# Gated mix of an S5 scan and an H3 convolution on one core: half-width trigonometric tables, another order of the first chunk, and the last rows by column halves

## The chip, the cores and the metric

The kernel runs on one core of a Trainium2 chip. The metric is the device time of one execution in microseconds. A run lists one time per execution; the time of a kernel is the median of its runs. Beside the timed runs there is one profiled execution, with the start, the duration and the waits of every instruction.

The core has five engines that run side by side and meet through semaphores: PE (matrix products, with PEld for its weight loads), DVE (elementwise), ACT (activation functions and scaled copies), POOL (small setup, and the issue of accumulating DMAs) and SP (issue of the other DMAs). Each engine takes its instructions in the order in which they were written down for it.

## What is computed

Inputs have 2048 rows (time) and 1024 columns (features), in bf16. Two branches are computed from the same `x` and mixed by a gate per row:

```python
g = sigmoid((x * gate_w).sum(-1, keepdims=True))

# branch A: a diagonal complex state space, P = 1024 states
Lam = Lambda_re + 1j * Lambda_im
Lam_bar = exp(exp(log_dt) * Lam)
B_bar = ((Lam_bar - 1) / Lam)[:, None] * (B_re + 1j * B_im)
Bu = einsum("bld,pd->blp", x, B_bar)
h[t] = Lam_bar * h[t - 1] + Bu[t]
a = 2 * einsum("blp,dp->bld", h, C_re + 1j * C_im).real + x * Dskip

# branch B: four taps on k, times v, a long convolution with ssm_k, a skip, times x
kv = (sum over t of shifted k * shift_k) * v
y = irfft(rfft(kv, 2L) * rfft(ssm_k, 2L))[:L] + kv * ssm_D
b = x * y

out = g * a + (1 - g) * b
```

## The kernel before, in words

All five engines' orders are written out by hand. Every operation goes through `put` (line 98) and so has line 100 in the profile; groups are told apart by the names of their tiles.

**Branch B** goes through 8 chunks `c` of 128 features. For a chunk, `load("kT", c)`, `load("v", c)` and `load("kn", c)` fetch `k` transposed, `v`, and the filter `ssm_k` transposed. `dgs` builds four diagonal matrices from the tap weights (tile `dg`, one buffer); for chunk 0 they are `dg0`, on DVE. `taps` (or `first_times_v` for chunk 0) makes 64 small matmuls against them in two PSUM halves, `times_v` multiplies by `v` into `ks`. `mirror` reverses `ks` in time on PE, from which DVE makes an even part `ev` and an odd part left in `ks`. Then `fwd_K` and `fwd_V` transform the filter and `ks` by matmuls against tables of cosines and sines: `KC` and `KS_` (four 128-row tiles by 512 columns) for the filter, `CF` and `SF` (two by 512) for `ks`. The 512 columns are frequencies and are taken as four blocks `fi` of 128. `overlap` and `products` (or `mid_products`) form the spectrum `G` on DVE, with some sums done by accumulating DMAs (`gather`). `inverse` turns `G` back (PSUM tiles `psz` and `low`) and stores the chunk in DRAM (`cv_scr`). A chunk's inverse is done in the next chunk's turn. `add_skip` adds `ssm_D` to the first row of the filter tile `kn`.

**Branch A**: `state_params` computes the small columns from `log_dt` and `Lambda`; its four steps are put between other work by `step(sp)`. `Bu` steps (PSUM `bu`) are spread over the chunks to fill PE. After the chunks come 16 scan steps (`scan`), with `Cy_g` (PSUM `psy`) for the output products.

**Tables.** A table's value is the cosine or sine of 2 pi times a product of a row number and a column number. `kernel_table(h)` makes the product `a` for 256 columns of all four tiles, removes whole turns by adding and subtracting `MAGIC` (`r`), and ACT takes sine, absolute value and cosine. `kA = kernel_table(0)` comes first of all, `kB = kernel_table(1)` later, in steps between the work of chunk 0. `CF` and `SF` come from `hf` and `rqf` at full width.

**Start.** ACT issues the six small row DMAs (tap weights `skr`, three A parameters `prow`, `gwr`, `sD`). PE turns these rows to columns by small matmuls into the PSUM tile `p`, with idle products (`raise_clock`, tile `raised`) around them. SP issues, in this order: `kT` of chunk 0 first half, `v` first half, `kT` second half, `v` second half, `kn` of chunk 0. PSUM holds four tiles of this size in all, given out in turn, so a matmul may have to wait until ACT or DVE has read an older tile.

**Buffers of loads.** `kT`, `v` and `kn` of all chunks share four buffers, so a load waits until an older chunk's tile has been used. SP issues in order, so a load that waits holds those behind it. `load_BT(0, ...)`, the first B matrices of branch A, stand behind `kT` of chunk 2.

**End.** The last four row tiles share one loop (lines 1235 to 1247). Each has a PSUM tile of two halves of 512 columns; for each tile PE makes the last eight matmuls, and then DVE adds the gate's part and SP stores 1024 columns. For one of them ACT scales and DVE adds; the last tile's matmuls go by halves and it is stored in two halves.

Of the kernel before, what the change touches and what calls it, by code (L numbers as in the profile page):

```python
# [9 lines left out]
ALU = mybir.AluOpType  # L10
# [10 lines left out]
def kernel(  # L21
# [26 lines left out]
    nc = tc.nc  # L48
# [126 lines left out]

    nc.scalar.dma_start(out=skr, in_=B_shift_k.rearrange("(j p) k -> j p k", p=128))
    for i, ap in enumerate((A_log_dt, A_Lambda_re, A_Lambda_im)):
        nc.scalar.dma_start(out=prow[i * ND:(i + 1) * ND, :], in_=ap.rearrange("(j p) -> j p", p=128))
    nc.scalar.dma_start(out=gwr, in_=gate_w.rearrange("(j p) -> j p", p=128))
    pih = consts.tile([128, 1], F32, name="pih")  # L180
# [5 lines left out]
    put("act", nc.scalar.activation, out=one, in_=magic, func=ACT.Sin, scale=0.0)  # L186
    nc.scalar.dma_start(out=sD, in_=B_ssm_D.rearrange("(o d) -> o d", o=1))

# [30 lines left out]
    put("pool", nc.gpsimd.memset, kT0[:, 0:PAD], 0.0)  # L219
    for h in range(2):  # L220
        hs, ns = slice(h * S // 2, (h + 1) * S // 2), slice(h * NT // 2, (h + 1) * NT // 2)
        load_t(kT0[:, PAD + hs.start:PAD + hs.stop], kf[hs, 0:128])
        move(v0[:, ns, 0], vf.rearrange("(n p) d -> p n d", p=128)[:, ns, 0:128])
    lds["kT", 0], lds["v", 0] = kT0, v0[:, :, 0]
    load("kn", 0)

# [39 lines left out]
    colk_i = iota_i32([128, 4], [[128, 4]], 0, 1, "colk")  # L266
    fr_i = iota_i32([128, 512], [[4, 512]], 1, 0, "fr_")
    ident = consts.tile([128, 128], BF16, name="ident")
# [27 lines left out]
    ts(colk, colk_i, 1.0 / 2048.0, None, ALU.mult)  # L296
    fr_ = room[:, 0:512]
    copy(fr_, fr_i)

    def kernel_table(h):  # L300

        hs = slice(h * 256, (h + 1) * 256)
        a, r = early([128, 4, 256], F32, "ka"), early([128, 4, 256], F32, "kr")
        for q in range(4):
            ts(a[:, q], fr_[:, hs], colk[:, q:q + 1], None, ALU.mult)
            ts(r[:, q], fr_[:, hs], colk[:, q:q + 1], MAGIC, ALU.mult, ALU.add)
            if q == 1:
                yield
        put("dve", V.scalar_tensor_tensor, out=flat(r), in0=flat(r), scalar=-MAGIC, in1=flat(a), op0=ALU.add,
            op1=ALU.subtract)  # L310
        yield
        act(KS_[:, :, hs], r, func=ACT.Sin, scale=-TWO_PI)
        act(a, r, func=ACT.Abs)
        yield
        act(KC[:, :, hs], a, func=ACT.Sin, bias=pih, scale=-TWO_PI)

    pcol = consts.tile([128, 3 + KS, ND], F32, name="pcol")
    gwb = consts.tile([128, ND], BF16, name="gwb")
    psp = ps2([128, 2, 512], "p")
    raise_clock(3)  # L320
    for k in range(KS):
        mm(psp[:, 1, k * ND:(k + 1) * ND], skr[:, :, k], ident[32:32 + ND, 32:32 + ND], True, True)
    raise_clock(5)
    mm(psp[:, 0, 0:3 * ND], prow, ident[64:64 + 3 * ND, 64:64 + 3 * ND], True, True)
    mm(psp[:, 1, KS * ND:(KS + 1) * ND], gwr, ident[32:32 + ND, 32:32 + ND], True, True)
    raise_clock(2)
    kA = kernel_table(0)
    steps(kA, 2)
    hf, rqf = early([128, 1024], F32, "h"), early([128, 1024], F32, "rq")
    for mt in range(2):  # L330
        ts(hf[:, mt * 512:mt * 512 + 512], fr_, colm[:, mt:mt + 1], None, ALU.mult)
    copy(pcol[:, 3:], psp[:, 1, 0:KS * ND].rearrange("p (i j) -> p i j", j=ND))
    dg0 = ks_pool.tile([128, KS, 128], BF16, name="dg", bufs=1)
    for k in range(KS):
        ts(dg0[:, k], ident, pcol[:, 3 + k, 0:1], None, ALU.mult)

    def dgs(c, on_dve=False):
# [179 lines left out]
    def first_times_v(c, dg):  # L517

        kT, v = lds.pop(("kT", c)), lds.pop(("v", c))
        ks = kss[c] = ks_pool.tile([128, 4, 4, 128], BF16, name="ks")  # L520
        for h in range(2):
            tt(of_blocks(ks, h), by_block(tap_sums(kT, dg, h)), by_block(v[:, 8 * h:8 * h + 8]), ALU.mult)
            yield
        lo = mirror(c)
        yield
        e = eo_pool.tile([128, 2, 4, 128], BF16, name="ev")
        tt(e, ks[:, 2:4], lo, ALU.subtract)
        tt(ks[:, 2:4], ks[:, 2:4], lo, ALU.add)
        eos["v", c] = e, ks[:, 2:4]

    def times_v(c):

        ks, v = kss[c], lds.pop(("v", c))
        tt(ks, ks, v.rearrange("p (b q) d -> p q b d", q=4), ALU.mult)
        yield
        lo = eo_pool.tile([128, 2, 4, 128], BF16, name="lo", tag="lo", bufs=2)
        act(lo, mirror(c), func=ACT.Copy)
        yield
        e = eo_pool.tile([128, 2, 4, 128], BF16, name="ev")
        tt(e, ks[:, 2:4], lo, ALU.subtract)  # L540
        if c == 1:
            tt(ks[:, 2:4], ks[:, 2:4], lo, ALU.add)
        else:
            gather(ks[:, 2:4], lo)
        eos["v", c] = e, ks[:, 2:4]
# [352 lines left out]

    def Cy_g(tb, tl, ps, g, last, by_half=False):
        t0 = HP + tl * 128  # L900
        tsl = slice(t0, t0 + 128)
        order = [(j, c, dh) for j in range(2) for c in range(2) for dh in range(2)]
        for j, c, dh in sorted(order, key=lambda o: o[2]) if by_half else order:
            mm(ps[dh], hbs[tb, g][:, c, j, tsl], CT[2 * g + j][:, c, dh * 512:(dh + 1) * 512],
               g == 0 and j == 0 and c == 0, last and j == 1 and c == 1)
# [26 lines left out]
    def finish(t_, ps=None):  # L932
# [4 lines left out]
        if t_ < NT - 4:  # L937
            ga = gas.pop(t_)
            gather(ga, xr)
            yield  # L940
        elif ps is None:
            yield
            ga = gas.pop(t_)
            tt(ga, ga, xr, ALU.add)
        else:
            yield
            ga = a_room(t_)
            for o, i in ps:
                put("dve", V.scalar_tensor_tensor, out=ga[:, o], in0=i, scalar=gcols[:, t_:t_ + 1], in1=xr[:, o],
                    op0=ALU.mult, op1=ALU.add)  # L950
                if len(ps) > 1:
                    move(of[rows, o], ga[:, o])
            if len(ps) > 1:
                return
        if t_ < NT - NG - 1:
# [5 lines left out]
    none = iter(())  # L961
    copy(pcol[:, 0:3], psp[:, 0, 0:3 * ND].rearrange("p (i j) -> p i j", j=ND))
    sp = state_params()
    run(kA)
    ts(rqf, hf, MAGIC, -MAGIC, ALU.add, ALU.add)
    tt(rqf, hf, rqf, ALU.subtract)
    act(flat(SF), rqf, func=ACT.Sin, scale=TWO_PI)
    act(hf, rqf, func=ACT.Abs)
    act(flat(CF), hf, func=ACT.Sin, bias=pih, scale=-TWO_PI)
    first = first_times_v(0, dg0)  # L970
    kB = kernel_table(1)
    turns = inverse_table()
    step(first)
    add_skip(0, True)
    step(first)
    fwd_K(0, (0,))
    dg1 = dgs(1)
    step(first)
    fwd_K(0, (1,))
    copy(gwb, psp[:, 1, KS * ND:(KS + 1) * ND])  # L980
    step(kB)
    run(first)
    step(kB)
    load("kT", 1)
    load("v", 1)
    load("kn", 1)
    fwd_V(0, (0, 1))
    step(kB)
    run(kB)
    taps(1, dg1)  # L990
    overlap(0, 0)
    p0 = products(0, 0)
    steps(p0, 3)
    dg = dgs(2, True)
    tv = times_v(1)
    step(tv)
    fwd_K(0, (2, 3))
    step(tv)
    add_skip(1, True)
    fwd_V(0, (2, 3))  # L1000

# [3 lines left out]
    for c in range(NC - 1):  # L1005
        n, nn = c + 1, c + 2
        if c == 0:
            load("kT", nn)
            load_BT(c, 0)
            load_BT(c, 1)  # L1010
            load_xT(0)
# [4 lines left out]
            fwd_K(n, (0, 1))  # L1016
            step(p0)
            run(tv)
            overlap(0, 1)
            step(p1)  # L1020
            step(sp)
            step(p1)
# [10 lines left out]
            dg = dgs(nn + 1)  # L1033
            run(p1)
            tv = times_v(nn)
            step(tv)
            add_skip(nn)
            Bu()
# [11 lines left out]
        if c == 2:  # L1050
            load_xT(1)
        step(prod)
        run(tv)
        step(prod)
        step(last)
# [175 lines left out]
    for tl in order:  # L1231
        ps = ps2([128, 2, 512], "psy")
        halves = [(slice(h * 512, h * 512 + 512), ps[:, h]) for h in range(2)]
        pss[tl] = [ps[:, 0], ps[:, 1]], halves if tl == order[-1] else [(slice(0, D), flat(ps))]
    for g in range(NG - 1):
        for tl in order:
            Cy_g(tb, tl, pss[tl][0], g, False)
    run(finish(t0 - 1))
    fins = {}
    for tl in order:  # L1240
        fins[tl] = finish(t0 + tl, None if tl == order[1] else pss[tl][1])
        step(fins[tl])
    for tl in order:
        Cy_g(tb, tl, pss[tl][0], NG - 1, True, tl == order[-1])
        if tl == order[1]:
            scale_a(t0 + tl, pss[tl][1])
        run(fins[tl])
# [28 lines left out]
```

## Time and profile before

| what | value |
|---|---|
| timed runs | 406.81, 404.75 and 406.56 us; median 406.56 |
| profiled execution | 392.88 us, its span 390.9 us |
| granted PE clock in it | 0.998 |
| DMA moved | 68.44 MB, mean 175 GB/s |
| DVE's longest idle before one kind of work in the chunks | `ks` waiting for ACT's `ks`: 3.4 us in 5 waits |

The span is the time from the first to the last instruction of the program. A timeline row gives the start, the duration, the engine, the operation with its output and input tiles, how many instructions were merged into the row, and in brackets how long the engine stood idle before it and what released it. Matmul durations contain their pipeline drain, so PE's pace is read from the distance between starts. Rows with `SPq`, `ACTq` or `POOLq` are issues of DMAs; the transfer goes on after them.

### The profile page before, as it was taken

To read this page: it belongs to the slowest core of one execution; us is meant where nothing else is said; L and a number is where in the kernel's file an instruction comes from. 1 tells how busy PE (TensorE), PEld (TensorE's weight loads), DVE (VectorE), ACT (ScalarE), POOL (GpSimd) and SP (SyncE) were. 2 spreads that over 40 slices of the span, in tenths; PEclk is the share of its full clock that TensorE was granted. 3 is DMA by queue.
4 is the path that set the end of the run, shared out by engine and by line. 5 is a ranking of instruction groups with operands and counts; after the bars stand their busy time and mean duration, and the time that the engine had idled before them with its cause. 6 is when DMAs were issued, how large, how long until landed. Compare 5 with 4: busy or idle time off the path is not lost.

```text
span 390.9 us, 6094 instructions
## 1 busy us (share of the span) xinstructions
PE 380.4 (97%) x2220; PEld 190.2 (49%) x2256; DVE 367.0 (94%) x543; ACT 306.1 (78%) x476; POOL 74.3 (19%) x101
## 2 busy tenths in 40 slices
PE   7999999999999999999999999999999999999995
PEld 4656564646446464444344444444444454444442
DVE  8899999899999999999999899999979999999964
ACT  4897879687777958684994698999787999898521
POOL 3010022211121222210100010101232334432400
PEclk9999999999999999999999999999999999999999
DMA  8669999999897965676999999677789999998754
GB/s 178 147 97 189 243 222 224 192 191 220 144 228 141 244 149 100 146 129 108 165 232 180 212 174 222 138 155 166 159 182 191 174 202 195 220 194 172 134 101 141
DMA packets 132527, 68.44 MB, mean 175 GB/s; under 512 B 114569, under 2 KB 117137, under 8 KB 132498
## 3 DMA queue, kind: packets, MB, share of 16 engines
q1 hardware_dynamic: 120640, 42.22, 51.4%
q0 software_dynamic: 11776, 25.83, 38.6%
q8 instruction: 17, 0.28, 0.3%
q14 instruction: 12, 0.10, 0.1%
q10 hardware_dynamic: 82, 0.02, 0.0%
HBM read 12.87 MB, written 8.39 MB: 54 GB/s over the span
## 4 chain that ended last, share of the span: by engine, by line
PE 55%; DVE 20%; issue 11%; DMA 5%; ACT 4%; POOL 3%; DVEq 0%; POOLq 0%
PE bu L100 14%; PE psk L100 11%; PE psy L100 9%; PE taps L100 7%; PE psz L100 6%; PE psv L100 6%; DVE P L100 5%; DMA pbb<-gd 3%; DVE R L100 2%; DMA BT<-in_A_B_im_dram 2%; DVE CT L100 2%; DVE U L100 2%; POOL ga L100 2%; DVE BT L100 1%; PE low L100 1%
## 5 line engine op out<-in xcount | busy, mean ns | idle before, releaser
L100 PE MATMUL bu<-xT,BT 128*128 128x512 bf16 x496 | 112.1, 379 | 1.2 <-DMA BT<-in_A_B_im_dram 0.5
L100 PE MATMUL psy<-CT,U 128*128 128x512 bf16 x501 | 110.6, 379 | 0.6
L100 PEld LDWEIGHTS <-BT 128*128 128x128 bf16 x512 | 49.7, 98 | 60.7 <-DMA BT<-in_A_B_im_dram 1.4
L100 PEld LDWEIGHTS <-U 128*128 128x128 bf16 x512 | 50.0, 98 | 59.9
L100 ACT ACTIVATE Q<-U,lam 128x512 bf16<-128x512 bf16 x64 | 37.2, 605 | 16.3 <-DVE U L100 14.7
L100 ACT ACTIVATE U<-bu 128x1024 bf16<-128x1024 f32 x32 | 31.6, 1015 | 12.3 <-PE bu L100 11.0
L100 ACT ACTIVATE R<-U,lam 128x512 bf16<-128x512 bf16 x64 | 37.2, 609 | 0.0
L100 PE MATMUL psk<-kn,KS 128*128 128x512 bf16 x128 | 32.9, 379 | 0.1
L100 PE MATMUL psk<-kn,KC 128*128 128x512 bf16 x128 | 32.8, 379 | 0.0
L100 DVE TENSOR_TENSOR_SCAN P<-r,init,P 128x256 bf16<-128x256 f32 x48 | 32.1, 730 | 0.2
L100 PEld LDWEIGHTS <-kT 128*128 128x128 bf16 x512 | 30.6, 101 | 2.9 <-issue 1.1
L100 PE MATMUL taps<-dg,kT 128*128 128x128 bf16 x512 | 31.4, 224 | 0.3 <-DVE dg L100 0.3
L100 ACT ACTIVATE Vh<-psv 128x1024 bf16<-128x1024 f32 x32 | 30.3, 1040 | 0.5 <-PE psv L100 0.5
L100 DVE TENSOR_TENSOR wkh<-KR,Vh 128x1024 bf16<-128x1024 bf16 (+4 forms) x27 | 29.4, 1097 | 1.0 <-DMA G<-wkh 1.0
L100 ACT ACTIVATE Kh<-psk 128x1024 bf16<-128x1024 f32 x16 | 16.2, 1020 | 7.4 <-PE psk L100 7.4
L100 ACT ACTIVATE BT<-psk 128x1024 bf16<-128x1024 f32 x16 | 16.1, 1019 | 6.3 <-PE psk L100 6.1
L100 DVE TENSOR_TENSOR R<-TCS,P 128x2048 bf16<-128x2048 bf16 x16 | 19.6, 1225 | 0.6
L100 DVE TENSOR_TENSOR U<-U,Q 128x1024 bf16<-128x1024 bf16 x26 | 17.8, 683 | 2.4 <-ACT Q L100 2.3
L100 POOL DMA_DIRECT2D G<-wkh x8 | 9.9, 1236 | 53.0 <-DVE wkh L100 34.2
L100 PEld LDWEIGHTS <-KC 128*128 128x128 bf16 x128 | 12.5, 98 | 15.2 <-ACT KC L100 0.3
L100 DVE TENSOR_TENSOR P<-TCS,R 128x2048 bf16<-128x2048 bf16 x16 | 19.5, 1220 | 0.3
L100 PE MATMUL psv<-ks,SF 128*128 128x512 bf16 x64 | 19.0, 379 | 0.6 <-DVE ks L100 0.5
(166 smaller groups left out, 639.8 us busy)
## 6 DMA issues: line engine op xcount, KB each, us to landing
G<-wkh POOLq DMA_DIRECT2D x7, 768.0 KB, 8.9
BT<-wkh POOLq DMA_DIRECT2D x6, 768.0 KB, 8.9
cv_scr<-sd SPq DMA_DIRECT2D x8, 512.0 KB, 3.5
pbb<-cv_scr SPq DMA_DIRECT2D x12, 256.0 KB, 3.2
xr<-in_A_x_dram SPq DMA_DIRECT2D x12, 256.0 KB, 5.3
pbb<-gd POOLq DMA_DIRECT2D x12, 256.0 KB, 4.5
v<-in_B_v_dram SPq DMA_DIRECT2D x5, 512.0 KB, 8.4
R<-R POOLq DMA_DIRECT2D x10, 256.0 KB, 4.5
```

The lines of the kernel that those rows point to most:

```text
L100: i = f(*a, **kw)
```

## The change

- **Tables.** Columns are made for the lower 256 only. Columns 256 to 511 follow from the lower ones: a column number that is 256 higher adds 1024 times four half steps to the phase, which for `KC` and `KS_` is a change of sign on odd rows, and for `CF` and `SF` turns the one into the other with such a sign. `alternating` makes the two sign columns `alt`, and four DVE multiplies write the upper halves. `kernel_table(k)` now takes two of the four tiles, `k1` with its products on ACT.
- **First chunk.** SP's order is `kT` both halves, `kn`, `v` both halves. The A rows and the gate row are fetched later, two after `hq` and two after `CF`, and are turned to columns behind `fwd_K` of chunk 0. `raise_clock` goes from 3, 5 and 2 around the small matmuls to 4, 8 and 2. `fwd_K` blocks 0 and 1 of chunk 0 come before its mirror, taps of chunk 1 before `fwd_V` blocks 0 and 1, then `fwd_K` block 2, the mirror of chunk 1, `fwd_K` block 3 and `fwd_V` blocks 2 and 3. `load_BT(0, ...)` moves ahead of `kT` of chunk 2.
- **Smaller moves.** In `first_times_v` both halves of the taps come before the first product. For chunk 2 `ks += lo` is a DVE add and no longer an accumulating DMA. One `step(sp)`, one `run(p1)` and one `run(tv)` change places.
- **Last rows.** For the last four tiles the final matmuls go by column halves, all four tiles' first halves and then all second halves; DVE does every tile, half by half, and SP stores eight halves.

```diff
+    def row(o, i):
+        put("act", nc.scalar.dma_start, out=o, in_=i)
...
-    for h in range(2):
+    for what, h in (("kT",0),("kT",1),("kn",0),("v",0),("v",1)):
...
-    fr_i = iota_i32([128, 512], [[4, 512]], 1, 0, "fr_")
+    fr_i = iota_i32([128, 256], [[4, 256]], 1, 0, "fr_")
...
+    def alternating():
+        ts(half, colk_i[:, 0:1], 0.5, None, ALU.mult)
+        ts(odd, half, MAGIC, -MAGIC, ALU.add, ALU.add)
+        tt(odd, half, odd, ALU.subtract)
+        tt(odd, odd, odd, ALU.mult)
+        ts(alt[:, 0:1], odd, -8.0, 1.0, ALU.mult, ALU.add)
+        ts(alt[:, 1:2], odd, 8.0, -1.0, ALU.mult, ALU.add)
+
+    def kernel_table(k):
+        qs = slice(2 * k, 2 * k + 2)
+        if k == 0:
+            both = early([128, 2, 2, 256], F32, "k0")
+            a, r = both[:, 0], both[:, 1]
+        else:
+            a, r = early([128, 2, 256], F32, "ka"), early([128, 2, 256], F32, "kr")
+            for q in range(2):
+                act(a[:, q], fr_, func=ACT.Identity, scale=colk[:, 2 + q:3 + q])
+            yield
+        for q in range(2):
+            if k == 0:
+                ts(a[:, q], fr_, colk[:, q:q + 1], None, ALU.mult)
+            ts(r[:, q], fr_, colk[:, 2 * k + q:2 * k + q + 1], MAGIC, ALU.mult, ALU.add)
...
-    raise_clock(3)
+    raise_clock(4)
     for k in range(KS):
         mm(psp[:, 1, k * ND:(k + 1) * ND], skr[:, :, k], ident[32:32 + ND, 32:32 + ND], True, True)
-    raise_clock(5)
-    mm(psp[:, 0, 0:3 * ND], prow, ident[64:64 + 3 * ND, 64:64 + 3 * ND], True, True)
-    mm(psp[:, 1, KS * ND:(KS + 1) * ND], gwr, ident[32:32 + ND, 32:32 + ND], True, True)
-    raise_clock(2)
+    raise_clock(8)
+    k0, k1 = kernel_table(0), kernel_table(1)
+    step(k1)
+    step(k0)
     copy(pcol[:, 3:], psp[:, 1, 0:KS * ND].rearrange("p (i j) -> p i j", j=ND))
     dg0 = ks_pool.tile([128, KS, 128], BF16, name="dg", bufs=1)
     for k in range(KS):
         ts(dg0[:, k], ident, pcol[:, 3 + k, 0:1], None, ALU.mult)
+    step(k0)
+    hq = early([128, 2, 2, 256], F32, "hq")
+    hf, rqf = hq[:, 0], hq[:, 1]
+    for mt in range(2):
+        act(hf[:, mt], fr_, func=ACT.Identity, scale=colm[:, mt:mt + 1])
+    for i, ap in enumerate((A_log_dt, A_Lambda_re)):
+        row(prow[i * ND:(i + 1) * ND, :], ap.rearrange("(j p) -> j p", p=128))
...
-        if c == 1:
+        if c < 3:
             tt(ks[:, 2:4], ks[:, 2:4], lo, ALU.add)
...
+    dg1 = dgs(1)
+    act(SF[:, :, lo_f], rqf, func=ACT.Sin, scale=TWO_PI)
     act(hf, rqf, func=ACT.Abs)
+    act(CF[:, :, lo_f], hf, func=ACT.Sin, bias=pih, scale=-TWO_PI)
+    row(prow[2 * ND:3 * ND, :], A_Lambda_im.rearrange("(j p) -> j p", p=128))
+    row(gwr, gate_w.rearrange("(j p) -> j p", p=128))
+    alternating()
     first = first_times_v(0, dg0)
-    kB = kernel_table(1)
     turns = inverse_table()
     step(first)
+    raise_clock(2)
     add_skip(0, True)
     step(first)
+    step(first)
+    ts(CF[:, :, hi_f], SF[:, :, lo_f], alt[:, 1:2], None, ALU.mult)
+    ts(SF[:, :, hi_f], CF[:, :, lo_f], alt[:, 0:1], None, ALU.mult)
     fwd_K(0, (0,))
-    dg1 = dgs(1)
+    fwd_K(0, (1,))
     step(first)
-    fwd_K(0, (1,))
-    copy(gwb, psp[:, 1, KS * ND:(KS + 1) * ND])
-    step(kB)
+    for tab in (KS_, KC):
+        ts(tab[:, :, hi_f], tab[:, :, lo_f], alt[:, 0:1], None, ALU.mult)
     run(first)
-    step(kB)
     load("kT", 1)
     load("v", 1)
     load("kn", 1)
+    load_BT(0, 0)
+    load_BT(0, 1)
+    p0 = products(0, 0)
+    tv = times_v(1)
+    taps(1, dg1)
     fwd_V(0, (0, 1))
...
-    for tl in order:
-        Cy_g(tb, tl, pss[tl][0], NG - 1, True, tl == order[-1])
-        if tl == order[1]:
-            scale_a(t0 + tl, pss[tl][1])
-        run(fins[tl])
+    for h in range(2):
+        for tl in order:
+            Cy_g(tb, tl, pss[tl], NG - 1, True, (h,))
+            step(fins[tl])
```

## The prediction

> **What bounds the kernel now.** I read the page first, then busy time in stretches of 10 us, then the timelines of PE, DVE, ACT and SP over the first 30 us, and last the places where PE waits.
>
> ```profile
> PE 380.4 (97%) x2220; PEld 190.2 (49%) x2256; DVE 367.0 (94%) x543; ACT 306.1 (78%) x476; POOL 74.3 (19%) x101
> ```
>
> ```profile
> 0.00:10.00 10.00, 8.00 (x41) 4.16 (x42) 8.54 (x25) 4.99 (x6) 3.89 (x17) 1.00 0.86 179
> 10.00:20.00 10.00, 9.45 (x93) 6.27 (x92) 8.76 (x16) 8.07 (x12) 0.00 (x0) 1.00 0.65 139
> 20.00:30.00 10.00, 9.65 (x76) 5.48 (x75) 9.58 (x18) 9.81 (x11) 1.62 (x3) 1.00 0.77 114
> ...
> 180.00:190.00 10.00, 8.81 (x41) 3.74 (x40) 9.90 (x8) 7.03 (x11) 1.33 (x2) 1.00 1.03 143
> ```
>
> The columns behind the second time are busy us of PE, PEld, DVE, ACT and POOL. PE is the bound: of its 10.5 idle us 2.9 lie in the first 30 us and 1.2 at 180 to 190. So time can be won where PE starts late or idles early, and at the tail. How PE starts:
>
> ```profile
> 1.19 1.46 PE L100 MATMUL raised<-wkh 128*128 128x512 bf16 x3 [1.19 <-DVE magic L100]
> ...
> 2.84 2.31 PE L100 MATMUL raised<-wkh 128*128 128x512 bf16 x5
> ...
> 5.89 1.03 PE L100 MATMUL raised<-wkh 128*128 128x512 bf16 x2
> 7.23 5.24 PE L100 MATMUL taps<-dg,kT 128*128 128x128 bf16 x64 [0.31 <-DVE dg L100]
> 12.31 1.03 PE L100 MATMUL psk<-kn,KS 128*128 128x512 bf16 x4
> 13.18 1.03 PE L100 MATMUL psk<-kn,KC 128*128 128x512 bf16 x4
> ...
> 17.29 0.59 PE L100 MATMUL psv<-ks,SF 128*128 128x512 bf16 x2 [0.50 <-DVE ks L100]
> ...
> 18.58 3.74 PE L100 MATMUL taps<-dg,kT 128*128 128x128 bf16 x64
> 22.16 1.03 PE L100 MATMUL psk<-kn,KS 128*128 128x512 bf16 x4
> ...
> 28.22 1.03 PE L100 MATMUL psk<-kn,KS 128*128 128x512 bf16 x4
> ```
>
> The first 64 taps take 5.08 us to the next start (12.31 - 7.23), the second 64 only 3.58 (22.16 - 18.58, 0.056 each). Two psk rows start 0.87 apart, 0.216 for a 512-column matmul, but a `raised` of the same size takes about twice that (2.31 / 5 less its drain, 0.43, so 0.107 for a tap): PE works at half rate at first, though the clock column, last but two in the rows by stretch, says 1.00. With n slow taps, 0.107 n + 0.056 (64 - n) = 5.08 gives 29 of them, and the full rate comes at 7.23 + 3.1, near 10.3. By the same 0.216 a fi of fwd_K (8 matmuls) is 1.73, one of fwd_V (4) 0.86, a mirror (2) 0.43.
>
> Taps wait for DVE's `dg`, and `dg` for this queue:
>
> ```profile
> 1.62 0.43 DVE L100 CAST room<-fr__i 128x512 f32<-128x512 int32 x1
> 2.08 0.35 DVE L100 TENSOR_SCALAR ka<-room,colk 128x256 f32<-128x256 f32 x1
> ...
> 4.32 0.34 DVE L100 TENSOR_SCALAR kr<-room,colk 128x256 f32<-128x256 f32 x1
> 4.70 1.23 DVE L100 SCALAR_TENSOR_TENSOR kr<-kr,ka 128x1024 f32<-128x1024 f32 x1
> ...
> 6.63 0.18 DVE L100 COPY pcol<-p 128x32 f32<-128x32 f32 x1
> 6.93 0.74 DVE L100 TENSOR_SCALAR dg<-ident,pcol 128x128 bf16<-128x128 bf16 x4
> ```
>
> **The change, part by part. Start of the taps.** Ahead of `dg` there now stand a room cast of half the columns (0.2 us less), four ts instead of eight (2.62 us from 2.08 to 4.70 become 1.3), one 512-column scalar_tensor_tensor (1.23 becomes 0.6), the pcol copy, and no h, which moves to ACT behind it. So 1.85 + 1.3 + 0.6 + 0.2 puts the first `dg` near 4.1 and the last near 4.9. PE's own queue is later than that: 4 raised from 1.19 end at 2.9, the four small p at 3.1, 8 raised at half rate 3.4 us on, at 6.5 (four p take 0.2: 1.19 + 1.46 to 2.84). Taps start at 6.5 instead of 7.23: 0.7 won. The p for the A rows and the gate, which stood in the gap of the rows between 5.15 and 5.89, leaves this place.
>
> **Rate of the taps.** PE is now busy without a break from 1.19. Before, 4 us of raised (1.19 to 5.15) did not free the rate, and 5.89 to 10.3 with a gap of 0.31 in it did. Bounds: freed no earlier than in that profile, at 10.3, 36 taps run at 0.107 and 28 at 0.056, and taps end at 11.9; freed by 6.5, they take 3.58 and end at 10.1. I take 10.1: an unbroken stretch of 5.3 us ahead of the taps is longer than either stretch above. Worth 5.08 - 3.58 = 1.5 us, or 0.3 lost at the other end.
>
> On this the Trainium skill (TensorE: Matmul & The Clock Gate, Part 1: The HAM clock gate) says that the full clock is given after one busy window of about 3.4 us, and that the windows run free of the kernel's start. By it the release falls between 4.6 and 8.0 us after this change, the taps end between 9.1 and 10.8, and an estimate of the gain moves by up to 1 us either way from run to run; the row of the first taps agrees that the time is not a matter of matmul count.
>
> **From the taps to 28.22.** The same work stands in another order: two raised at full rate (0.43), four fi of psk (6.92), two mirrors (0.86), 64 taps (3.58), four fi of psv (3.45), the small p (0.15): 15.4 us. With no wait this ends at 25.5, where before it ended at 28.22: 2.7 us won: 0.7, 1.5, and 1.1 of waits (28.22 - 7.23 less 5.08 and the psk, mirror, taps and psv above) less the 0.6 of raised and p. I went through the waits of each step.
>
> ```profile
> 0.74 1.26 SPq L100 DMA_TRANSPOSE kT<-in_B_k_dram  x1
> 2.06 0.56 SPq L100 DMA_DIRECT2D v<-in_B_v_dram  x1
> 2.68 1.86 SPq L100 DMA_TRANSPOSE kT<-in_B_k_dram  x1
> ...
> 5.22 2.28 SPq L100 DMA_TRANSPOSE kn<-in_B_ssm_k_dram  x1
> ...
> 13.77 3.51 SPq L100 DMA_TRANSPOSE kn<-in_B_ssm_k_dram  x1
> 22.40 1.91 SPq L100 DMA_TRANSPOSE kT<-in_B_k_dram  x1
> 24.35 5.13 SPq L100 DMA_TRANSPOSE BT<-in_A_B_re_dram  x1
> 29.52 3.16 SPq L100 DMA_TRANSPOSE BT<-in_A_B_im_dram  x1
> ```
>
> ```profile
> v<-in_B_v_dram SPq DMA_DIRECT2D x2, 256.0 KB, 3.9
> ```
>
> Loads: kT's second half is issued by 3.9 (1.86 from 2.0) and kn by 6.2, where it was 7.5; v's halves (0.56 each) go at 6.2 and 6.8 and land 3.9 later, at 10.1 and 10.7. psk of chunk 0 needs kn and the lower table columns only, so it can fill 10.5 to 14.0 while DVE multiplies by v (two at 1.23, done by 12.5) and mirror follows at 14.0. v's slack is 1.5 us.
>
> ```profile
> 7.99 1.15 ACT L100 ACTIVATE KC<-ka,pih 128x1024 bf16<-128x1024 f32 x1
> ...
> 14.24 1.02 ACT L100 ACTIVATE BT<-psk 128x1024 bf16<-128x1024 f32 x1 [1.40 <-PE psk L100]
> 15.16 1.27 ACT L100 ACTIVATE dg<-ident,pcol 128x128 bf16<-128x128 bf16 x4
> ```
>
> ACT: its table calls shrink to half columns (1.15 to some 0.6), the lower kernel tables are ready before 9.1, where KC's row ended. Then `dg` of chunk 1 waits for the taps of chunk 0, since dg has one buffer; behind it in ACT's queue stand SF, CF, two row DMAs and the psk evictions. So dg 10.2 to 11.5, SF and CF to 13.3, the DMAs (0.56 each at most, by SP's v row) to 14.4, first eviction done 15.4. The second half of taps(1) needs that PSUM slot at 16.3: slack 0.9 us. DVE's upper halves are four sign multiplies of bf16, for which no row exists; 0.18 (a quarter of the dg row) to 1.2 (the f32 row at 4.70) each, I take 0.35, nearer the dg row, which is bf16 too. They end near 14.6, the two parity steps (1.2 each by that row) at 17.0, and psv starts at 18.1: at 1.2 each they would cost PE about 2 us. Every cost of this paragraph is nothing while those slacks hold.
>
> SP later: BT0's two loads move ahead of kT(2). With kn at 12.5 to 16.0 they take 8.3 (5.13 + 3.16) to 24.3, kT(2) is out at 26.2 and lands at the latest 3.3 after (v's 3.9 less its 0.56), at 29.5. PE's taps(2) now stand at 25.5 + 3.5 = 29: nothing by the middle of that landing, 0.5 by its end.
>
> **Does the gain survive to the end?** DVE is 94% busy. Its own head wins less: it multiplies chunk 1 by v when ACT has evicted taps(1), 19.2, then come that product, three of chunk 0, dg and the two copies, 6.2 us, so `wkh<-BT,Vh` stands near 25.4 and not at 26.07. I compared DVE with PE in each chunk:
>
> ```profile
> DVE ks L100 <- ACT ks L100: 3.4, 5, 1.2
> ```
>
> ```profile
> 26.07 0.94 DVE L100 TENSOR_TENSOR wkh<-BT,Vh 128x1536 bf16<-128x1536 bf16 x1
> ...
> 78.53 2.35 DVE L100 TENSOR_TENSOR G<-G,BT 128x2048 bf16<-128x2048 bf16 x2
> ...
> 165.40 2.36 DVE L100 TENSOR_TENSOR G<-G,BT 128x2048 bf16<-128x2048 bf16 x2
> ```
>
> ```profile
> 83.46 1.03 PE L100 MATMUL psz<-G,CI 128*128 128x512 bf16 x4
> ...
> 168.00 1.03 PE L100 MATMUL psz<-G,CI 128*128 128x512 bf16 x4
> ```
>
> DVE waits five times for taps that PE and ACT have still to give, 3.4 us in all. If PE comes 2.7 us earlier these waits shrink, so DVE catches up: about 0.6 from its head and 2 from these by 83, against which stands the one `ks += lo` of chunk 2 (0.6) that was a DMA. psz has 2.6 us of slack against G at 83 and 0.24 at 168, so PE can keep at most what DVE regains. I take all 2.7 as kept, near 0 and 2.7 being the ends.
>
> **Tail.**
>
> ```profile
> 386.28 1.41 DVE L100 SCALAR_TENSOR_TENSOR BT<-psy,gcols,BT 128x512 bf16<-128x512 f32 x2 [0.42 <-PE psy L100]
> ```
>
> Both halves of the last tile are done after the last matmul, 1.41 us. Now seven of eight halves are done beside PE (0.7 against a group of 0.86), and one is left: 0.7 won. PE's second-half matmuls gain a wait for DVE, but each first half is read two groups before. ACT's scale_a goes; eight stores for five cost SP issues 0.86 apart, not at the end.
>
> Sum: 2.7 + 0.7 = 3.4 of the 392.88 of the profiled execution (span 390.9), so 389.5. The three timed runs lie at 404.75 to 406.81, 3.4% above it, for which the page shows no reason; I carry the same us over: 406.56 - 3.4 = 403.2.
>
> **Rivals.** *DVE becomes the bound* (11%): its busy 94% and the 0.24 us of slack speak for it, the five waits on taps against it. PE keeps only 0.6, with the tail 1.3: 405.2. *The rate is freed no earlier* (10%): 1.8 less (11.9 for 10.1), 405.0; the 4 us of raised that did not free it speak for it. *A load turns into a wait; slower* (13%): BT0's two transposes now stand ahead of kT(2) in SP's queue. Every us that kT(2) lands after 29 stops PE, so once the BT issues take 3 us more than their 8.3 the whole gain is gone, and beyond 5 more the kernel is slower by 0.5%; at 14 us (5.7 more) PE stops for 6.2 and the kernel takes 2.8 more than before: 409.4. For it: the BT rows took 5.13 and 3.16 while other loads ran beside them. Against it: the DMA share, last but one in the rows by stretch, was 0.65 and 0.77 at 10 to 30 us, where these loads now run. *The upper halves or v late* lies between and is held by the range.
>
> **How the numbers follow.** The forecast has 66%, its own range 401.5 to 405. About 0.5% (2 us) is what a measurement of this kernel can tell from no change. Faster by more: 62% from the forecast and 6% from the first two rivals, 68%. Within: 4 and 15, 19%. Slower: 13%. The range takes in the first two rivals and the spread of the timed runs (1.8 below the median): 400.5 to 406.6; it leaves the load rival out.
>
> **What would show it.** Taps start at 6.5 and take 3.6; PE's 28.22 row (first psk of chunk 1) stands near 25.5; no PE wait on ks, CF or kT before 30; DVE's ks waits shrink below 2 us; psz stands 2.7 earlier at 83 and at 168; after the last matmul one 512-column step of 0.7. A PE gap before taps(2), a psz wait on G, or taps at 0.107 us would show the rivals and make the prediction wrong.

## The result and the profile after

The changed kernel took 390.01 us (median of 6, 388.71 to 398.31), the kernel before 400.35 us (median of 6, 393.23 to 406.81; the three shown ahead of the prediction are among them). The ratio is 0.9874 with a 95% interval of 0.9837 to 0.9911, so the change makes the kernel 1.3% faster. The forecast was 403.2 us, a ratio of 0.9917, with a range from 400.5: the direction and most of the mechanism came out, the time lies far below the range.

Some executions take 5 to 30 us longer and are left out of the ratios (17 of 46 of the kernel before beside the experiments on one chip, none of 13 on another); the changed kernel's profiled one (398.31 us, span 396.4) is of this kind, and its trace shows a transfer that comes far too late.

Up to 130 us that trace shows nothing of it. Its timeline of PE (start, duration, output and inputs, instructions):

```profile
1.19 1.89 PE L100 MATMUL raised<-wkh 128*128 128x512 bf16 x4 [1.19 <-DVE magic L100]
...
3.24 2.64 PE L100 MATMUL raised<-wkh 128*128 128x512 bf16 x8
5.71 3.74 PE L100 MATMUL taps<-dg,kT 128*128 128x128 bf16 x64
9.29 0.59 PE L100 MATMUL raised<-wkh 128*128 128x512 bf16 x2
9.72 1.03 PE L100 MATMUL psk<-kn,KS 128*128 128x512 bf16 x4
...
17.18 0.59 PE L100 MATMUL psv<-ev,CF 128*128 128x512 bf16 x2
...
24.73 1.03 PE L100 MATMUL psk<-kn,KS 128*128 128x512 bf16 x4
...
28.19 3.74 PE L100 MATMUL taps<-dg,kT 128*128 128x128 bf16 x64
```

After 1.19 no row of these has a bracket: PE does not wait. Taps start at 5.71, not at 7.23, and take 3.58 (9.29 - 5.71) instead of 5.08; the first psk of chunk 1 stands at 24.73 instead of 28.22. The eight idle products take 2.47 where eight at half rate would take 3.46 and at full rate 1.73: some 3.4 were slow, so the full rate (0.216 us for a 512-column product instead of 0.43) came at 3.24 + 3.4 times 0.432, at 4.7. VectorE's timeline of the same stretch:

```profile
9.19 2.35 DVE L100 TENSOR_TENSOR ks<-taps,v 128x1024 bf16<-128x1024 f32 x2 [0.95 <-DMA v<-in_B_v_dram]
11.46 0.34 DVE L100 TENSOR_SCALAR CF<-SF,alt 128x512 bf16<-128x512 bf16 x1
12.66 0.35 DVE L100 TENSOR_SCALAR SF<-CF,alt 128x512 bf16<-128x512 bf16 x1 [0.85 <-ACT CF L100]
12.93 0.48 DVE L100 TENSOR_SCALAR KS<-KS,alt 128x1024 bf16<-128x1024 bf16 x1
13.32 0.48 DVE L100 TENSOR_SCALAR KC<-KC,alt 128x1024 bf16<-128x1024 bf16 x1
...
24.36 0.94 DVE L100 TENSOR_TENSOR wkh<-BT,Vh 128x1536 bf16<-128x1536 bf16 x1
```

The four sign multiplies are the new rows of half a microsecond or less; `wkh<-BT,Vh` stands at 24.36 and not at 26.07.

Then the late transfer, in the same execution, in PE's timeline and in busy time by stretches (after the second time: busy us of PE, PEld, DVE, ACT, POOL; PE clock; DMA share; GB/s):

```profile
135.47 3.74 PE L100 MATMUL taps<-dg,kT 128*128 128x128 bf16 x64
146.65 1.89 PE L100 MATMUL psk<-kn,KS 128*128 128x512 bf16 x4 [7.45 <-DMA kn<-in_B_ssm_D_dram]
148.33 1.91 PE L100 MATMUL psk<-kn,KC 128*128 128x512 bf16 x4
```

```profile
134.00:139.00 5.00, 5.00 (x72) 4.18 (x70) 5.00 (x5) 2.85 (x3) 0.89 (x1) 1.00 1.45 56
139.00:146.00 7.00, 0.20 (x4) 0.03 (x1) 0.79 (x1) 1.02 (x1) 1.22 (x1) 0.66 0.97 200
146.00:151.00 5.00, 4.35 (x11) 1.61 (x12) 4.68 (x5) 0.72 (x1) 0.00 (x0) 0.50 0.83 159
```

With the DMA engines busy, only 56 GB/s are moved; PE stands for 7.45 us, and four products then take 1.7 instead of 0.86, at a granted clock of 0.50. The stop and the half rate behind it make up nearly all of the 10 us between this span and the 386.4 of the same kernel below.

### The profile page after: what moved, and what is told of

It is laid out like the page before. It is cut to its first block, busy times and chain, and to the rows that moved or that the text cites. A ratio compares the mean times of both kernels' runs of the same rounds, so it can differ in the third digit from the quotient of the medians.

```text
span 396.4 us, 6147 instructions
## 1 busy us (share of the span) xinstructions
PE 382.8 (97%) x2260; PEld 189.9 (48%) x2260; DVE 365.4 (92%) x545; ACT 302.8 (76%) x479; POOL 73.6 (19%) x100
## 4 chain that ended last, share of the span: by engine, by line
PE 75%; DVE 12%; DMA 10%; issue 2%; SPq 1%; POOL 0%; DVEq 0%; POOLq 0%
PE psy L100 28%; PE bu L100 21%; PE psk L100 9%; DMA kn<-in_B_ssm_D_dram 5%; PE taps L100 5%; PE psv L100 4%; PE psz L100 3%; DMA G<-wkh 3%; DVE wkh L100 3%; DVE G L100 3%; DVE BT L100 3%; DMA BT<-in_A_B_im_dram 2%; PE raised L100 1%; PE low L100 1%; PE p L100 1%
## 5 line engine op out<-in xcount | busy, mean ns | idle before, releaser
L100 PE MATMUL psk<-kn,KS 128*128 128x512 bf16 x128 | 34.5, 394 | 7.4 <-DMA kn<-in_B_ssm_D_dram 7.4
L100 PE MATMUL psk<-kn,KC 128*128 128x512 bf16 x128 | 33.7, 387 | 0.0
L100 PEld LDWEIGHTS <-kT 128*128 128x128 bf16 x512 | 29.2, 98 | 2.0 <-DMA kT<-in_B_k_dram 0.3
L100 PE MATMUL taps<-dg,kT 128*128 128x128 bf16 x512 | 29.9, 219 | 0.0
L100 PEld LDWEIGHTS <-KS 128*128 128x128 bf16 x128 | 12.6, 101 | 22.2 <-DMA kn<-in_B_ssm_D_dram 7.6
```

The costliest lines, as they stand in the source:

```text
L100: i = f(*a, **kw)
```

## The experiments

Each ratio is to the kernel before, run beside the experiment. The first version with fewer idle products and the three with moved loads ran on a second chip, the others on one chip.

**Both kernels again.** Neither program is changed.

> The kernel before, unchanged, against itself. If its first times (404.75 to 406.81) were a disturbance that is not the kernel's, it takes 393 to 396 here and its ratio to itself is 1.00 within 0.5%; taps of chunk 0 start at 7.2 and the first psk of chunk 1 at 28.2 again. If 404 to 407 is its own time, it shows that here too, without a long wait of PE in the profile.

> The changed kernel, unchanged. Theory (3.5 us won ahead of the first psk of chunk 1, kept to the end, and 0.6 behind the last matmul): 4.1 us less than before, ratio 0.9896; the 7.4 us stop of PE at a psk of its first profile is gone, and psz starts stay 3.5 ahead up to 168. Rival (DVE takes part of the gain back behind 130 us, which the disturbed profile hid): psz of the last chunks only 1 to 2 us ahead, ratio 0.993 to 0.996.

Before: 395.09 us (ratio 0.9981, 0.9928 to 1.0034), profiled span 390.8. After: 388.8 us (0.9829, 0.978 to 0.9878), span 386.4, with no late transfer in it. So the median of the kernel before is 395 here and not 404 to 407, and its trace shows no long wait of PE. The last rows of PE before, and of PE and VectorE in the changed kernel:

```profile
361.69 24.55 PE L100 MATMUL psy<-CT,U 128*128 128x512 bf16 x111
```

```profile
375.70 6.85 PE L100 MATMUL psy<-CT,U 128*128 128x512 bf16 x30
376.55 6.79 DVE L100 SCALAR_TENSOR_TENSOR BT<-psy,gcols,BT 128x512 bf16<-128x512 f32 x8 [0.17 <-PE psy L100]
```

PE ends at 382.55 and VectorE 0.79 later, where it was 1.45 (387.69 less 386.24); from PE's end to the span's end it is 3.85 us instead of 4.66. PE's rows by which its lead is read:

```profile
5.41 3.74 PE L100 MATMUL taps<-dg,kT 128*128 128x128 bf16 x64
...
24.43 1.03 PE L100 MATMUL psk<-kn,KS 128*128 128x512 bf16 x4
...
79.66 1.03 PE L100 MATMUL psz<-G,CI 128*128 128x512 bf16 x4
...
178.05 1.68 PE L100 MATMUL bu<-xT,BT 128*128 128x512 bf16 x7 [0.74 <-DMA BT<-in_A_B_im_dram]
```

So the 4.5 us between the spans (390.9 - 386.4) are: 3.8 up to the first psk of chunk 1 (28.22 - 24.43), all of it still there at 83.46 against 79.66; 0.8 at the tail; and 0.1 given back. The timed ratio says more, 1.7% or 6.8 us. The times of the kernel before scatter upward from its profiled execution (392.0 to 398.8 us in this ratio), those of the changed kernel less (388.1 to 391.1); what the kernel before loses in its longer ones was not caught in a trace.

**The last rows alone, and all but the last rows.**

```diff
 only the last rows (kernel before)
+    for h in range(2):
+        for tl in order:
+            Cy_g(tb, tl, pss[tl], NG - 1, True, (h,))
+            step(fins[tl])
```

> The kernel before with only the last rows by column halves. Theory: 0.6 us less, ratio 0.9985; from the last matmul to the end 4.0 us and not 4.6. Rival (eight stores for five, and PE's new waits for DVE in the second halves, eat it): ratio 1.000 or above.

> The changed kernel with the last rows as before. Theory: 3.5 us less than before, ratio 0.991. Rival (the tail carries the gain): ratio above 0.996.

The last rows alone: 392.67 us, 0.9937 (0.9901 to 0.9974), span 390.4. Without them: 390.14 us, 0.9851 (0.9801 to 0.9902), span 388.9. In the trace of the first, PE ends 0.2 us later than before (at psz it stands 0.36 behind, 83.82, since the full rate came later), and the span still ends 0.5 earlier: from PE's end to the span's end it is 3.99 us instead of 4.66, so the tail alone is worth 0.7, as the theory has it. The trace of the second kept both late 512-column steps:

```profile
384.24 1.41 DVE L100 SCALAR_TENSOR_TENSOR BT<-psy,gcols,BT 128x512 bf16<-128x512 f32 x2 [0.42 <-PE psy L100]
```

The parts add up within their intervals; the timed ratio of the tail alone is larger than 0.7 us accounts for, which I put down to the scatter named. Without the tail the span gains 2.0 us where the theory had 3.5: in that trace the full rate came at 7.4, and psz stands only 2.2 ahead.

**Idle products.** In the changed kernel 8 become 2; in a second version the last 2 go as well.

```diff
-    raise_clock(8)
+    raise_clock(2)
...
-    raise_clock(2)
+    raise_clock(0)
```

> The changed kernel with two idle products between the tap-weight columns and the taps instead of eight. Theory (the full rate comes 3 to 6 us after PE's first product, whatever PE does in that time, so cold taps are as good as idle products): taps start near 4.7 when dg is there, run partly at half rate, and end 0.7 to 1.0 earlier; first psk of chunk 1 near 23.5 to 25, 0.7 less than the changed kernel. Rival (the eight products free the rate, and without them or with a pause ahead of the taps it comes at 8 or later): taps end no earlier, 0 to 1 us more than the changed kernel.

> The changed kernel with 4, 2 and 0 idle products instead of 4, 8 and 2: the taps follow as soon as VectorE has the first dg and take the place of the idle products. Theory (products at half rate do no harm when they are the taps themselves, idle ones only push the taps back): the taps start near 4.3, the first psk of chunk 0 at 8.4 to 8.7 where kn has landed, the first psk of chunk 1 at 23.4 to 23.8 instead of 24.4 to 24.7, and the kernel takes 0.7 to 1.3 us less than the changed one (ratio against the kernel before 0.980 to 0.985). Rival (with fewer products ahead the full rate comes later): the taps run at half rate to their end near 11 and the gain is given back, ratio 0.985 to 0.990.

With 4, 2 and 2: 387.96 us, 0.9827 (0.9764 to 0.9891), span 385.3; with 4, 2 and 0: 391.06 us, 0.9893 (0.9827 to 0.996), span 386.5. PE of the one and of the other:

```profile
4.34 4.00 PE L100 MATMUL taps<-dg,kT 128*128 128x128 bf16 x64
...
23.68 1.03 PE L100 MATMUL psk<-kn,KS 128*128 128x512 bf16 x4
```

```profile
4.34 4.33 PE L100 MATMUL taps<-dg,kT 128*128 128x128 bf16 x64
...
13.73 3.75 PE L100 MATMUL taps<-dg,kT 128*128 128x128 bf16 x64 [1.26 <-DMA kT<-in_B_k_dram]
```

With fewer idle products the taps start at 4.34 and not at 5.41, and in the first version PE is 0.75 us further at chunk 1 than in the trace above (24.43). That trace does not show slow taps taking the place of idle products: only its first four taps stand further apart, 0.11 to 0.16 us, since VectorE starts its four `dg` 0.16 apart, and from 4.78 on they are 0.056 apart. In the second version six taps from 4.84 on are 0.107 apart, and the full rate still comes at 5.5: there taps at half rate did no harm to the rate. But `kT` of chunk 1 landed 6.8 us after its issue, against 5.0 in the first version, in which PE reaches taps(1) at the same time and does not wait. The 1.26 us eat the gain, and the first psk of chunk 1 stands at 24.87, not at the 23.4 to 23.8 of the theory. By the times neither is proved better than the changed kernel; the first is the fastest by its trace.

**Loads.** In the changed kernel `v` goes ahead of `kn` again; `load_BT(0, ...)` goes behind `kT` of chunk 2 again; or `xT(0)` too goes ahead of that `kT`.

```diff
-    for what, h in (("kT",0),("kT",1),("kn",0),("v",0),("v",1)):
+    for what, h in (("kT",0),("v",0),("kT",1),("v",1),("kn",0)):
...
-    load_BT(0, 0)
-    load_BT(0, 1)
...
+    load_xT(0)
```

> The changed kernel with the first loads in the order of before (kT, v, kT, v, kn). Theory (kn first lets psk fill the time until v is multiplied): kn lands some 2 us later, near 10, the first psk waits 0.3 to 1 us for it, and the first psk of chunk 1 is that much later. Rival (the order of the loads is worth nothing, both land in time): no wait of PE, same times.

> The changed kernel with BT0's two loads behind kT of chunk 2 again. Theory (the loads for the first bu step would end where they did before, near 38 to 40, while PE is there at 39.3): bu waits 0.5 to 3 us for BT or xT, and the gain shrinks by that. Rival (BT0's place is worth nothing): no wait of PE ahead of bu, the time of the changed kernel within 0.3 us.

> The changed kernel with the two loads of xT(0) also ahead of kT of chunk 2, to measure the slack of that load. The slower rival of the prediction (a load ahead of kT of chunk 2 stops PE one for one): kT is issued 6 to 8 us later, at 26 to 28, taps of chunk 2 wait 2 to 5 us behind 27.9, and the kernel takes 2 to 5 us more than the changed one. If kT has more slack than the 2 us that its issue at 19.5 to 22.1 suggests, the taps wait less than 1 us.

The first two: 389.59 us (0.9879, 0.9826 to 0.9932; span 387.8) and 389.51 us (0.9871, 0.9816 to 0.9926; span 388.4). The first adds a PE wait of 0.59 us for `kn`, as its theory has it. In the second the wait of the theory, ahead of the first `bu` near 39, did not come. PE waits for a `BT` once, much later:

```profile
179.88 1.68 PE L100 MATMUL bu<-xT,BT 128*128 128x512 bf16 x7 [1.30 <-DMA BT<-in_A_B_im_dram]
```

This is the row at 178.05 above, and its wait lies between nothing and 1.42 us in the other traces, those of the kernel before among them. So the place of BT0's loads shows no price; PE is later in this trace because the full rate came late, at 6.7. No order of these loads makes or breaks the change. The third took 396.25 us (1.0047, 1.0013 to 1.0081): slower than before. SP and PE in it:

```profile
16.90 3.01 SPq L100 DMA_TRANSPOSE BT<-in_A_B_im_dram  x1
19.95 5.55 SPq L100 DMA_TRANSPOSE xT<-in_A_x_dram  x2
25.61 5.50 SPq L100 DMA_TRANSPOSE kT<-in_B_k_dram  x1
```

```profile
27.16 1.03 PE L100 MATMUL psk<-kn,KC 128*128 128x512 bf16 x4
33.34 6.14 PE L100 MATMUL taps<-dg,kT 128*128 128x128 bf16 x64 [5.15 <-DMA kT<-in_B_k_dram]
39.31 1.03 PE L100 MATMUL psk<-kn,KS 128*128 128x512 bf16 x4
```

```profile
28.00:33.00 5.00, 0.19 (x1) 0.00 (x0) 4.90 (x12) 1.56 (x4) 0.00 (x0) 0.86 1.23 182
33.00:38.00 5.00, 4.67 (x44) 4.67 (x45) 5.00 (x7) 1.02 (x1) 0.00 (x0) 0.50 1.15 284
```

`kT` of chunk 2 is issued by 31.1 and not by 22.4. PE stands 5.15 us, and then 64 taps take 5.97 instead of 3.58, at a clock of 0.50: a wait of 5.15 costs 7.5, more than the 2 to 5 us expected.

**The tables alone, and their multiplies twice.** The kernel before with half-width tables only; and the changed kernel with each sign multiply written twice.

```diff
 the tables alone (kernel before; cut)
-    kB = kernel_table(1)
+    ts(CF[:, :, hi_f], SF[:, :, lo_f], alt[:, 1:2], None, ALU.mult)
+    ts(SF[:, :, hi_f], CF[:, :, lo_f], alt[:, 0:1], None, ALU.mult)
...
 the multiplies twice (changed kernel; the pair for CF and SF is doubled too)
-    for tab in (KS_, KC):
+    for tab in (KS_, KC, KS_, KC):
         ts(tab[:, :, hi_f], tab[:, :, lo_f], alt[:, 0:1], None, ALU.mult)
```

> The kernel before with nothing but the half-width tables: lower 256 columns are made, four sign multiplies write the upper halves; loads, order of the first chunk and last rows stay. Theory (the order of the first chunk makes most of the head's gain, the tables alone only shorten VectorE's part): the first taps start near 6.9 instead of 7.23 behind the same gap for the late rows, still run at half rate to about 10, and the waits for ks shrink, so the first psk of chunk 1 stands at 27.0 to 28.0 instead of 28.22 and the kernel gains 0.3 to 1.3 us (ratio 0.997 to 0.999). Rival (the tables make the gain, the order only spends it): the first psk of chunk 1 stands near 25.5 and the kernel gains 2.5 us or more (ratio below 0.994).

> The changed kernel with each of the four sign multiplies written twice (the second writes the same values again): 0.34 + 0.35 + 0.48 + 0.48 = 1.65 us more on VectorE between 11.6 and 13.5 us. Theory (the upper halves have about 1.3 us of slack, since the odd part ks is done at 16.0 and TensorE takes it at 17.3): one TensorE wait for ks of 0.3 to 0.6 us near 17.3, VectorE's later waits of 1.1 and 0.6 us are used up, and the kernel is 0.3 to 0.8 us slower than the changed one (ratio against the kernel before 0.983 to 0.989). Rival (VectorE is the bound by now): all 1.65 us are lost, seen as later psz rows at 80 and 164, and the ratio is 0.987 to 0.991.

Tables alone: 393.63 us, 0.9967 (0.9937 to 0.9998), but a profiled span of 391.7. In its trace the first taps start at 6.62 and the first psk of chunk 1 stands at 26.56, further than the first theory had it, since the full rate came early, and short of the rival's 25.5. Of these 1.7 us PE loses 0.8 to a wait for `kT` at 49.7, so 0.7 is left at psz (82.77), and the rest goes to waits for `BT` (1.41, in the row where before it is 0.46) and ACT's `ga` (0.5): without the new order of the first chunk the tables are worth little. Multiplies twice: 389.18 us, 0.9881 (0.9861 to 0.99), span 387.2. PE has no wait for `ks`, against my 0.3 to 0.6; that execution got its full rate late, at 6.3, so PE was 1.1 us later, and ks (done at 18.28) came 0.1 ahead of its use at 18.39. The rows, VectorE's first:

```profile
17.06 1.22 DVE L100 TENSOR_TENSOR ks<-ks,mirror 128x1024 bf16<-128x1024 bf16 x1
```

```profile
18.39 0.59 PE L100 MATMUL psv<-ks,SF 128*128 128x512 bf16 x2
```

The multiplies cost PE nothing in the changed kernel, and doubled they still are when the rate comes late; what doubling costs when it comes early was not seen.

**PE kept busy in the kernel before.**

```diff
-    raise_clock(5)
+    raise_clock(7)
...
-    raise_clock(2)
+    raise_clock(3)
```

> The kernel before with 3, 7 and 3 idle products around the small matmuls instead of 3, 5 and 2, which fill the 0.50 and 0.31 us in which TensorE stood idle at 5.3 and 6.9. Theory (the full rate comes once a stretch of some 3.4 us without such a gap is over, at a time between 4 and 8 us that changes from run to run): the first taps start at 7.2 to 7.4 and run at full rate from the start or soon after, ending at 11.0 or earlier instead of 12.3; the first psk of chunk 1 stands at 26.9 to 27.6 and the kernel gains 0.6 to 1.5 us (ratio 0.996 to 0.9985). Rival (the rate comes at a fixed time or after a fixed amount of work and the gaps do not matter): the taps end at 12.2 to 12.7 as before and the kernel gains nothing (ratio 0.999 to 1.001).

394.57 us, 0.998 (0.9942 to 1.0019). Its start:

```profile
2.84 3.03 PE L100 MATMUL raised<-wkh 128*128 128x512 bf16 x7
...
5.93 0.82 PE L100 MATMUL raised<-wkh 128*128 128x512 bf16 x3
7.23 4.05 PE L100 MATMUL taps<-dg,kT 128*128 128x128 bf16 x64 [0.48 <-DVE dg L100]
11.12 1.03 PE L100 MATMUL psk<-kn,KS 128*128 128x512 bf16 x4
```

Seven products at 0.43, then three at 0.22: the full rate comes by 5.9 and the taps end at 11.1 instead of 12.3, as the first theory has it; one trace fits it and does not prove it, as the comparison of the starts below shows. The gain is 1.2 us at psz (82.28) but not at the end. VectorE's and PE's rows further on:

```profile
134.48 1.23 DVE L100 TENSOR_TENSOR wkh<-KR,Vh 128x2048 bf16<-128x2048 bf16 x1 [4.79 <-DMA G<-wkh]
```

```profile
143.03 1.02 PE L100 MATMUL psk<-kn,KS 128*128 128x512 bf16 x4 [1.53 <-ACT sd L100]
...
169.75 1.04 PE L100 MATMUL psz<-G,CI 128*128 128x512 bf16 x4 [0.65 <-DVE G L100]
```

A gather that lands late stops VectorE for 4.8 us. PE then waits 1.53 us for ACT's `sd`, which ACT can only take up once VectorE has summed it, and 0.65 for `G`: what PE wins is lost again where a transfer comes late.

**All the starts side by side.** The moment of the full rate is the first entry in each trace's record of the granted clock. Where PE's products run on across it, the distances between them change within 0.1 us of it.

| kernel | PE idle in its start | full rate at | first psz of the row at 83.46 |
|---|---|---|---|
| before; again; last rows only | 0.50 and 0.31 | 10.25; 10.32; 10.99 | 83.46; 83.49; 83.82 |
| tables only | 0.67 at 5.1 | 4.75 | 82.77 |
| before, kept busy | 0.48 at 6.8 | 5.60 | 82.28 |
| changed; again | none | 4.76; 4.17 | 79.97; 79.66 |
| all but last rows | none | 7.44 | 81.26 |
| 4, 2, 2; 4, 2, 0 | none | 4.28; 5.49 | 78.91; 80.10 |
| `v` first; BT late; xT ahead | none | 5.05; 6.74; 4.26 | 80.84; 80.92; 87.51 |
| multiplies twice | none | 6.35 | 80.74 |

In the ten traces in which PE ran on from 1.19 until the full rate was there, it came at 4.17 to 7.44. Of the four in which PE stood idle between 5 and 6 us, as in this row of the kernel before, three got it after 10:

```profile
5.78 0.18 PE L100 MATMUL p<-ident,rows 8*128 8x8 bf16 x1 [0.50 <-DMA rows<-in_gate_w_dram]
```

The fourth, the tables alone, got it at 4.75, ahead of its gap; its five products behind 2.81 take 2.19 where they took 2.31 before, and the two behind the gap run at full rate:

```profile
2.81 2.19 PE L100 MATMUL raised<-wkh 128*128 128x512 bf16 x5
...
5.78 0.17 PE L100 MATMUL p<-ident,rows 8*128 8x8 bf16 x1 [0.67 <-DMA rows<-in_gate_w_dram]
5.89 0.61 PE L100 MATMUL raised<-wkh 128*128 128x512 bf16 x2
```

Up to there PE does the same work as in the kernel before. So the gap does not hold the rate back in every execution, and the kernel before may get it early at times too: 3.8 us is the gain against traces of it that got it late.

## Why the prediction was wrong, and where it was right

**The step that failed** is the last one: "I carry the same us over: 406.56 - 3.4 = 403.2". The sum against the profiled execution ended at 389.5, and the changed kernel took 390.01 and 388.8. The three runs on the other side were not the kernel's ordinary time: its medians were 396.14, 394.51 and 395.82 beside the three groups of experiments. The prediction had noted that the page shows no reason for their 3.4% and kept them all the same. What made these three longer no trace shows. The 7.45 us stop of the changed kernel and the 4.8 us stop of VectorE above are the two traced examples of what can; that the three had the like is argued from these. That the sum of 389.5 lies so near the measured medians is partly luck, since its head term was too small, as follows.

**Start and rate of the taps.** The 2.7 us of the head became 3.8 and 3.5 in the two traces of the changed kernel. The mis-sized term is the moment of the full rate: I had it come by 6.5, after eight idle products at half rate, and it came at 4.17 and 4.76, so that those products ran faster and the taps started at 5.41 and 5.71. Where it came at 6.35 and 6.74 in the table, psz stands 2.7 and 2.5 ahead, just the sum predicted. So 2.7 is right for one point of a spread from 4.17 to 7.44, in which each microsecond of delay costs half of one. The Trainium skill (TensorE: Matmul & The Clock Gate, Part 1: The HAM clock gate) gives a busy window of about 3.4 us that runs free of the kernel's start; the width found, 3.3 us, agrees with it, and this sentence in the prediction was nearer than its sum. The ends do not quite agree: 4.17, 4.26 and 4.28 lie ahead of the 4.6 that the prediction worked out from that window.

One reading of the prediction needs a correction that leaves its sum as it is. Not all of the 1.5 us that the taps were to win is rate: before, the first three distances between taps are 0.16 us, the pace of VectorE's `dg`, which is some 0.2 us more than half rate alone. That wait went too, since `dg` is now ready ahead of PE.

**Waits of the head.** None came: `v` kept VectorE waiting 0.95 us and PE not at all, the multiplies took 0.34 to 0.48 for my 0.35, and `kT(2)` left SP by 22.4 and not 26.2, since the BT issues took 4.3 us together and not 8.3.

**Does the gain survive.** Yes, but for the 0.1 us given back, and not by the narrow margin feared. VectorE is ahead by 1.7 us at `wkh<-BT,Vh` where I gave its head 0.6, and its waits for ACT's `ks` fell from 3.4 to 2.2 us (the mark set was 2). In the view of waits of the changed kernel run again:

```profile
DVE ks L100 <- ACT ks L100: 2.2, 3, 1.1
```

The psz row that stood at 168.00 before stands at 164.19 there, still 3.8 ahead.

**Tail.** 0.8 for 0.7 (0.7 in the run of the last rows alone), with one 512-column step of 0.79 behind PE.

**Rivals.** *DVE becomes the bound* did not happen; PE waits for no VectorE work after the start. *The rate is freed no earlier* is refuted by the table: at 7.44 at the latest in the changed start, against 10.25 in the profile that the prediction read. *A load turns into a wait* did not happen in this order, but the mechanism is real: one more load ahead of `kT(2)` gave a wait of 5.15 us. Its price was too low in the prediction, which charged a microsecond for each one waited; half rate afterwards adds 2.4 to these 5.15. The Trainium skill (TensorE: Matmul & The Clock Gate, Why this matters for your kernels) warns of gaps of PE above some 3 us, and the runs agree: 5.15 and 7.45 us were followed by a clock of 0.50, gaps of 1.53 us and less inside the kernel were not. Gaps between 1.53 and 5.15 us were not seen.

Left open: why the transfers crawl in some executions, and whether the change makes that rarer. Dropping ssm_D's own transfer, which PE waited for, was not tried. The new order of the first chunk without the half-width tables, and the smaller moves one by one, were not run, so what each is worth is known only by what is left when the rest is taken away. How much idle time the start bears before the rate comes late stays open as well.

## What to carry to other kernels

Forecast a ratio, or the time of the execution whose trace was read, and do not add a gap between times and trace that nothing explains. In a start at half rate, put useful work in the place of idle products, and keep the stretch unbroken; expect its gain to vary from run to run, here by some 1.6 us. Price a late load at its wait plus the half rate behind it, and see whether the engine next to the bound wins as much as the bound does.

## What was not expected of the hardware

The clock column reads 1.00 over the half-rate start (0 to 10 us: 1.00 in both kernels), while after a stop inside a kernel it reads 0.50. The record of the granted clock behind it has its first entry only where the full rate comes (10.25 us before, 4.76 after), and the column counts the time ahead of it as 1.00: at the start the rate must be read from distances between rows. With the DMA engines busy for a whole stretch (share 1.45), 56 GB/s were moved where the changed kernel's other execution moved 246 between the same times.
